# Loading the shared weight pieces of a recurrent memory transformer from a scratch with long rows

## The chip, the cores and the metric

The kernel runs on one core of one Trainium2 chip. The metric is the device time in microseconds of one execution; the median of three runs is given. Engines are named as in the profile: PE (TensorE, matmuls), PEld (its weight loads), DVE (VectorE), ACT (ScalarE), POOL (GpSimd), SP (SyncE, which here only issues transfers).

## The reference

Two branches are mixed by a gate. Branch A walks through the 2,048 tokens in 64 segments of 32; each segment attends to itself and to 8 memory rows, and the first 8 rows of its output are the next segment's memory, so that the segments form a chain. Branch B is a GEGLU layer.

```
g = sigmoid((x * gate_w).sum(-1))
for s in range(64):                       # branch A, Dm = 1024, 32 heads of 128
    h = concat([mem, x[32*s : 32*s+32]])  # 8 + 32 rows
    q, k, v = h @ Wq, h @ Wk, h @ Wv      # each 1024 x 4096
    p = softmax(mask(q k^T / sqrt(128)))
    o = (p v) @ Wo                        # 4096 x 1024
    mem, out_s = o[:8], o[8:]
b = (gelu(x @ w_gate) * (x @ w_up)) @ w_down
return g * a + (1 - g) * b
```

All tensors are in bfloat16. Wk, Wq, Wv and Wo hold 8 MB each, together 32 MB, which is more than the on-chip memory has: part of them has to be read again in every segment.

## The kernel before

**Steps and pieces.** A step is one segment. Each of the four weights is cut in 16 pieces of 512 KB, (m, u, i): m is the weight (k, q, v, o), u the half of the heads, i one of eight blocks (for k, q and v 128 rows of the contraction; for o a block of four heads and half of the columns). A piece fills one slot of 4,096 bytes in each of 128 partitions (`sl` for k, q, v, `wall` for o). A step does its projections in two rounds, r = 0 with half u = s % 2 and r = 1 with the other half; the next step starts with the half that this one ended with.

**Shared slots.** Most pieces have a slot of their own and are loaded once. Fourteen slots are shared by the two halves of a block (`PAIRS`, L313: k 0 and 1, q 0 and 1, v 0 to 4, o 0, 1, 4, 5, 6). A shared slot holds the half that r = 0 uses; when that use is over (`spent`, L440), the other half is loaded for r = 1 of the same step, and stays for r = 0 of the next. So each step loads 14 pieces, 7 MB.

**Loads in groups.** Where neighbouring slots come free together, one transfer loads them (`GROUPS`, L408: k 0-1, q 0-1, v 0-1, v 2-3, o 4-6); it goes out when the last of the group is spent (`load_group`, L420). Pieces of k, q and v come from the inputs, where a piece's row is 4,096 contiguous bytes of a row of 8,192. Pieces of Wo come from the input in rows of 1,024 bytes at first. In steps 1 to 10 `keep` (L383, called at L932) stores one shared piece of Wo in each step from its slot into a scratch in DRAM; from then on it is read from there, pieces 0 and 1 alone in rows of 4,096 bytes (`wo_scr`), pieces 4 to 6 as a group in rows of 12,288 (`wg_scr`).

**Order.** The order of the work is written out by hand. `walk` (L330) is the order of the projections: k0 (first half of its blocks), q0 (two), the second half of o1 of the step before, q0 (two), v0, k0, q0, v0, then k1, q1, o0, v1 and the first half of o1. `plan` (L899) hangs everything else on places of that list with `on(m, r, n, ...)`, which means: before block n of m in round r. At ("o", 1, 0) stand, among others, the attention of the second half, SP's load of qkr (rows of q and k of tokens that were projected ahead, L540) and SP's store of oRc (part of the attention's output, L985). All weights, hT (next inputs, L531), the stores of `keep` and these two go through SP's queue in program order, and an instruction of SP that waits holds those behind it. POOL issues smaller transfers on a queue of its own. Every instruction waits on semaphores that `_Prog` (L31) derives from which one writes and reads which bytes: a load into a slot waits for the last matmul that used it and for a store that reads it.

**Fills.** Rows that do not depend on the memory are projected ahead for four steps at a time (`fill`, L842, matmuls of L850): two such projections in each of two steps out of four, one in the two others, none in the last five. In steps with two, ACT copies the second result to a stage called 0S or 1S (L661), which lies on the same bytes as hT and oRc, so that this copy waits for the store of oRc to have landed.

**After step 63** the rest of Wo's products follow (L1027), and then branch B in four blocks of 512 tokens (L1068 on).

Of the kernel before, what the change touches and what calls it, by code (L numbers as in the profile page):

```python
# [5 lines left out]
BF16 = mybir.dt.bfloat16  # L6
# [24 lines left out]
class _Prog:  # L31
# [47 lines left out]
    def op(self, eng, fn, rd=(), wr=(), lane=None, after=()):  # L79
        o = _Op(eng, fn)  # L80
        if lane is not None:
            ln = self.lanes.get(lane)
            if ln is None:
                ln = self.lanes[lane] = [self.new_sem(f"{self.name}_{lane}"), 0, None]
            if ln[2] is not None:
                o.deps.append(ln[2])
            ln[1] += 16
            o.sem, o.val, o.inc, o.need = ln[0], ln[1], 16, True
            ln[2] = o
        for r in rd:  # L90
# [12 lines left out]
        return o  # L103
# [107 lines left out]
def bass_gated_mix__memory_aug_recurrent_mem_tr__geglu_ffn__prompt_kernel(  # L211
# [16 lines left out]
    S, D = xf.shape  # L228
# [17 lines left out]
    with ExitStack() as es:  # L246
# [14 lines left out]
        v_scr = nc.dram_tensor("v_scr", [NSEG, NB, 16, 2, 128], BF16)  # L261
        o_scr = nc.dram_tensor("o_scr", [NSEG, 128, 256], BF16)
        a_scr = nc.dram_tensor("a_scr", [NSEG, 4, SEG, 256], BF16)
        wo_scr = nc.dram_tensor("wo_scr", [16, 128, 2048], BF16)
        wg_scr = nc.dram_tensor("wg_scr", [2, 128, 3, 2048], BF16)

        PB = [es.enter_context(nc.psum_tensor(f"pb{i}", [128, 512], FP32)) for i in range(8)]
        PBV = [p[:, :].bitcast(BF16) for p in PB]
# [5 lines left out]
        def al(name, shape, dt=BF16, at=None):  # L274
            if at is None:
                cur[0] = (cur[0] + 63) // 64 * 64
                t = _T(nc, name, shape, dt, cur[0])
                cur[0] += t.nb
                return t
            return _T(nc, name, shape, dt, at)  # L280
# [32 lines left out]
        PAIRS = {"k": (0, 1), "q": (0, 1), "v": (0, 1, 2, 3, 4), "o": (0, 1, 4, 5, 6)}  # L313
# [33 lines left out]
        sl = al("sl", [128, nkqv, 2048])  # L347
# [11 lines left out]
        op = P.op  # L359
# [3 lines left out]
        def src(k):  # L363
            m, u, i = k
            if m == "o":
                h0 = 16 * u + 4 * (i % 4)
                return A_Wo[h0:h0 + 4, :, 512 * (i // 4):512 * (i // 4) + 512].rearrange("h p f -> p h f")
            W = {"q": A_Wq, "k": A_Wk, "v": A_Wv}[m]
            return W[i * 128:(i + 1) * 128, 16 * u:16 * u + 16, :].rearrange("d h e -> d (h e)")

        def dst(t, k):
            return t[:, :].rearrange("p (h f) -> p h f", h=4) if k[0] == "o" else t[:, :]

        kept = set()
        wo_at = lambda k: wg_scr[k[1], :, k[2] - 4, :] if 4 <= k[2] < 4 + 3 else wo_scr[8 * k[1] + k[2]]

        def load_piece(t, k, lane):
            if k in kept:
                op("sp", lambda e: e.dma_start(t[:, :], wo_at(k)), rd=[("D", "wo", k)], wr=[t.r()], lane=lane)
            else:  # L380
                op("sp", lambda e: e.dma_start(dst(t, k), src(k)), wr=[t.r()], lane=lane)

        def keep(k):  # L383
            t = slots[home[k]]
            op("sp", lambda e: e.dma_start(wo_at(k), t[:, :]), rd=[t.r()], wr=[("D", "wo", k)], lane="wo")
            kept.add(k)

        assert NSEG % 2 == 0
# [16 lines left out]
            if done[n] == 0 and uses[n][0] == k:  # L405
                fetch(n)

        GROUPS = {("k", 0): 2, ("q", 0): 2, ("v", 0): 2, ("v", 2): 2, ("o", 4): 3}  # L408
        lead = {(m, i + x): (m, i) for (m, i), n in GROUPS.items() for x in range(n)}
        for (m, i), n in GROUPS.items():  # L410
            assert all(home[m, 0, i + x] == home[m, 0, i] + x for x in range(n))
        held = {}

        def due(n):
# [5 lines left out]
        def load_group(k0, n):  # L420
            m, u, i = k0
            h = home[k0]
            t, x = (wall, h - nkqv) if m == "o" else (sl, h)
            reg = ("S", slots[h].off, slots[h].off + n * PIECE)
            if m == "o":
                op("sp", lambda e: e.dma_start(t[:, x:x + n, :], wg_scr[u]), rd=[("D", "wo", (m, u, i + y)) for y in range(n)],
                   wr=[reg], lane=f"sl{h}")
            else:
                W = {"q": A_Wq, "k": A_Wk, "v": A_Wv}[m]
                v = W[i * 128:(i + n) * 128, 16 * u:16 * u + 16, :].rearrange("(y p) h e -> p y (h e)", y=n)  # L430
                op("sp", lambda e: e.dma_start(t[:, x:x + n, :], v), wr=[reg], lane=f"sl{h}")
# [8 lines left out]
        def spent(k):  # L440
# [8 lines left out]
            q.append((n, *due(n)))  # L449
            if len(q) == GROUPS[g]:  # L450
                del held[g]
# [13 lines left out]
        for g in range(4):  # L465
            q = slice(32 * g, 32 * g + 32)
# [62 lines left out]
        def load_h(s, eng="sp"):  # L529
            t = hT[s % 2]  # L530
            op(eng, lambda e: e.dma_start(t[:, :, :].rearrange("p k c -> p (k c)"), xq_scr[s // 4, :, s % 4, :]),  # L531
               rd=[("D", "xq", s // 4)], wr=[t.r()], lane=f"h{eng}")
# [10 lines left out]
        def load_v(s, us=slice(0, 2), eng="pool"):  # L543
# [7 lines left out]
           wr=[gwb.r()], lane="gw")  # L551
# [3 lines left out]
        for n in range(8):  # L555
# [9 lines left out]
           rd=[memT.r()], wr=[hT0.r()])  # L565
# [328 lines left out]
        def fill0(m, r, b, st, G=0, h=hR):  # L894
            run(fill(m, r, b, h))
            fill_evac(m, r, G, b, st)
            fill_put(m, r, G, st)

        def plan(s):  # L899
            last = s == NSEG - 1  # L900
            ua, ub = s % 2, 1 - s % 2
# [6 lines left out]
            def on(m, r, n, *fs, s=s):  # L908
                at.setdefault((s, m, r, n), []).extend(fs)
# [18 lines left out]
                on("k", 0, 5, lambda: load_r(G))  # L928
            if not last and s == 0:
                on("k", 0, 4, lambda: load_h(s + 1))  # L930
            if 1 <= s <= 2 * len(PAIRS["o"]):
                on("k", 0, 4, lambda: keep(("o", s % 2, PAIRS["o"][(s - 1) // 2])))  # L932
            on("q", 0, 4, lambda: evac(bank_of["k", 0], stage["k"], "act"))
# [49 lines left out]
            if not last:  # L983
                on("o", 1, 0, lambda: load_qk(s + 1, 0, "sp"))
            on("o", 1, 0, lambda: op("sp", lambda e: e.dma_start(o_scr[s], oRc[:, :, :].rearrange("p c x -> p (c x)")),  # L985
                                     rd=[oRc.r()], wr=[("D", "o", s)], lane="sto"))
# [13 lines left out]
            if two:  # L1000
# [4 lines left out]
                                     wr=[("D", "a", s)], lane="st"), **nx)  # L1005

        for s in range(NSEG):
            plan(s)
        for _, e, m, r, n in walk:
# [6 lines left out]
           wr=[("D", "a", NSEG - 1)], lane="st")  # L1016

        load_oR(NBK - 1)
        for b in range(NBK):
            rb = rbs[b % 2]  # L1020
            for hf in range(2):
# [47 lines left out]
        for fb in range(NFB):  # L1069
            HB, DN = ((0, 1, 2, 3), (4, 5, 6, 7)) if fb % 2 == 0 else ((4, 5, 6, 7), (0, 1, 2, 3))  # L1070
            for j in range(NJ):
                c, cc = jch[j][0], jch[j][1] * 128
                bg, bu = HB[2 * (j % 2)], HB[2 * (j % 2) + 1]
                for bk, w in ((bg, wg[c]), (bu, wu[c])):
# [8 lines left out]
                t = tp[j % 2]  # L1083
# [4 lines left out]
                   rd=[BK(bg), s1.r()], wr=[t.r()])  # L1088
# [87 lines left out]
```

## Time and profile before

| | us |
|---|---|
| median of three runs | 2309.16 |
| lowest and highest | 2306.65, 2320.56 |
| the profiled execution, its own time | 2311.71 |
| its span, first to last instruction | 2309.9 |
| PE busy | 2069.2 |
| DVE busy | 1044.2 |
| ACT busy | 541.9 |
| POOL busy | 423.4 |
| first and last store of oRc (L985) | 124.1, 1657.8 |

The median of the runs is 0.1% below the profiled execution. A step is read from one store of oRc to the next. Median times from issue to landing: Wk's group 6.1 us, Wq's 9.0, Wv's 11.2, a single piece of Wo 6.2, Wo's group of three 9.5, the store of oRc 4.3. A transfer's time to landing holds its time in the queue; the time that it takes by itself is seen only where two land one behind the other. Besides the views that the prediction shows, the trace keeps a record of each packet that a DMA engine moved: queue, size and duration.

### The profile page before, as it was taken

What the parts mean: (1) busy time and instruction counts of PE and PEld (TensorE: products, weight loads), DVE (VectorE), ACT (ScalarE), POOL (GpSimd) and SP (SyncE); (2) the same over time, 40 slices, a digit from 0 to 9 for tenths busy, and PEclk for the clock granted to TensorE, in tenths of its full rate; (3) what the DMA queues carried; (4) which work ended last, traced back from release to release, by engine and by line L of the source; (5) the groups of instructions that cost most, each with busy time, mean ns of one, the idle gap of its engine ahead of it and who ended that gap; (6) DMA issues with size and microseconds to landing.
All of it is one profiled execution on the core that took longest, in us unless ns stands there. A gap on an engine that the chain in (4) does not pass through costs nothing.

```text
span 2309.9 us, 69920 instructions
## 1 busy us (share of the span) xinstructions
PE 2069.2 (90%) x31393; PEld 982.4 (43%) x31393; DVE 1044.2 (45%) x2697; ACT 541.9 (23%) x1111; POOL 423.4 (18%) x819
## 2 busy tenths in 40 slices
PE   4588888989999899898998989988799999999999
PEld 2243443444444444444444444443464444444444
DVE  3344444454444544445444444454315446163462
ACT  1122222222222222222222222221113123032130
POOL 4422212222222221222222222221100000000000
PEclk9699999999999999999999999998999999999999
DMA  9989999999999999999999989998964440803520
GB/s 370 358 299 336 327 337 347 324 341 334 330 346 328 347 322 327 344 318 352 322 340 339 331 313 328 324 344 313 331 214 139 153 148 10 291 19 128 167 88 19
DMA packets 237563, 638.04 MB, mean 276 GB/s; under 512 B 22441, under 2 KB 91305, under 8 KB 230481
## 3 DMA queue, kind: packets, MB, share of 16 engines
q1 hardware_dynamic: 213440, 596.58, 72.9%
q0 software_dynamic: 13888, 26.31, 3.5%
q10 hardware_dynamic: 9936, 10.69, 1.3%
q8 instruction: 247, 4.05, 0.7%
q14 instruction: 52, 0.42, 0.1%
HBM read 596.85 MB, written 36.63 MB: 274 GB/s over the span
## 4 chain that ended last, share of the span: by engine, by line
PE 56%; DMA 32%; DVE 5%; issue 3%; ACT 2%; POOL 1%; SPq 0%; ACTq 0%; POOLq 0%; DVEq 0%
PE pb L780 18%; PE pb L1077 15%; DMA sl<-in_A_Wv_dram 10%; DMA wall<-wg_scr 7%; PE pb L1131 5%; DMA qkr<-qk_scr 3%; PE pb L813 3%; DMA o_scr<-oRc 3%; PE pb L796 3%; PE pb L678 3%; PE pb L850 3%; PE pb L1027 2%; PE pb L1112 2%; DMA sl<-in_A_Wq_dram 1%; DMA xr_scr<-xr 1%
## 5 line engine op out<-in xcount | busy, mean ns | idle before, releaser
L780 PE MATMUL pb<-sl,hT 128*32 128x512 bf16 x12288 | 776.1, 385 | 36.6 <-DMA sl<-in_A_Wv_dram 17.3
L780 PEld LDWEIGHTS pb<-sl,hT 128*32 128x32 bf16 x12288 | 312.5, 97 | 361.4 <-DMA sl<-in_A_Wv_dram 39.8
L850 PE MATMUL pb<-sl,hR 128*32 128x512 bf16 x3072 | 220.7, 392 | 3.5 <-issue 2.9
L1077 PE MATMUL pb<-xT,wg 128*128 128x512 bf16 x896 | 211.7, 379 | 0.8
L1077 PE MATMUL pb<-xT,wu 128*128 128x512 bf16 x896 | 211.7, 379 | 0.0
L813 PE MATMUL pb<-wall,oT 128*32 128x256 bf16 x4056 | 154.1, 278 | 33.7 <-DMA wall<-wg_scr 10.5
L824 DVE COPY part<-pb 64x256 f32<-64x256 f32 x128 | 54.0, 422 | 256.8 <-PE pb L813 256.0
L661 ACT ACTIVATE kS<-pb 128x512 bf16<-128x512 f32 x127 | 75.8, 597 | 385.1 <-PE pb L780 363.7
L796 PE MATMUL pb<-wall,oT 128*32 128x512 bf16 x2048 | 150.4, 389 | 9.8 <-issue 2.9
L763 POOL COPY oRc<-oT 128x128 bf16<-128x128 bf16 x128 | 96.3, 752 | 339.9 <-DVE oT L664 336.8
L1131 PE MATMUL pb<-wd,GT 128*128 128x512 bf16 x672 | 146.6, 379 | 2.7 <-DMA wd<-in_B_w_down_dram 2.6
L1085 ACT ACTIVATE s<-pb 128x512 f32<-128x512 f32 x112 | 66.8, 596 | 313.4 <-PE pb L1077 313.4
L813 PEld LDWEIGHTS pb<-wall,oT 128*32 128x32 bf16 x4056 | 96.9, 97 | 95.8 <-ACT oT L661 25.8
L714 ACT ACTIVATE E<-pb 128x320 bf16<-128x320 f32 x128 | 56.0, 437 | 333.8 <-DVE pb L713 333.8
L1086 DVE SCALAR_TENSOR_TENSOR tp<-s,pb 128x512 f32<-128x512 f32 x112 | 76.9, 687 | 125.9 <-ACT s L1085 125.7
L1077 PEld LDWEIGHTS pb<-xT,wg 128*128 128x128 bf16 x896 | 87.2, 98 | 107.9 <-DVE GT L1093 3.7
L1077 PEld LDWEIGHTS pb<-xT,wu 128*128 128x128 bf16 x896 | 87.7, 98 | 105.7
L879 POOL COPY kT<-qkr 128x128 bf16<-128x128 bf16 x128 | 37.3, 291 | 491.0 <-DVE kT L664 229.4
L664 DVE COPY kT<-pb 128x512 bf16<-128x512 bf16 x128 | 54.4, 425 | 160.9 <-PE pb L678 160.9
L664 DVE CAST oT<-pb 128x160 bf16<-128x160 f32 x256 | 76.5, 320 | 104.4 <-PE pb L746 104.4
L726 DVE STREAM_TRANSPOSE tAB<-pAB 128x128 bf16<-128x128 bf16 x512 | 114.0, 280 | 4.4
L1090 DVE SCALAR_TENSOR_TENSOR tp<-tp,pb 128x512 f32<-128x512 f32 x112 | 77.0, 687 | 78.5 <-ACT tp L1089 78.5
(103 smaller groups left out, 2158.6 us busy)
## 6 DMA issues: line engine op xcount, KB each, us to landing
sl<-in_A_Wv_dram SPq DMA_DIRECT2D x128, 1024.0 KB, 11.2
wall<-wg_scr SPq DMA_DIRECT2D x53, 1536.0 KB, 9.5
sl<-in_A_Wk_dram SPq DMA_DIRECT2D x64, 1024.0 KB, 6.1
sl<-in_A_Wq_dram SPq DMA_DIRECT2D x64, 1024.0 KB, 9.0
wall<-wo_scr SPq DMA_DIRECT2D x120, 512.0 KB, 6.2
wd<-in_B_w_down_dram SPq DMA_DIRECT2D x42, 1024.0 KB, 5.5
sl<-in_A_Wv_dram SPq DMA_DIRECT2D x75, 512.0 KB, 11.4
wall<-in_A_Wo_dram SPq DMA_DIRECT2D x41, 512.0 KB, 7.9
```

The source lines that it names most:

```text
L661: op("act", lambda e: e.activation(o, i, ACTF.Copy), rd=rd, wr=wr)
L664: op("dve", lambda e: e.tensor_copy(o, i), rd=rd, wr=wr, after=after)
L726: return [op("dve", lambda e, c=c: e.transpose(tAB[:, c + 32 * k:c + 32 * k + 4 * w].rearrange("p (j x) -> p j x", j=4)[:, :, 0:32], pAB[: ...
L763: op("pool", lambda e: e.tensor_copy(oRc[:, :, 16 * u:16 * u + 16].rearrange("p c x -> p x c"), oT[:, :, :, 32:40].rearrange("p g j c -> p ...
L780: ins = e.matmul(PB[bk][32 * g:32 * g + 32, :], lhsT=h[:, i, :], rhs=w[:, g * 512:(g + 1) * 512], start=(n == 0), stop=(n == 7))
L796: ins = e.matmul(PB[XO][32 * g:32 * g + 32, :], lhsT=oT[:, j, x, 0:32], rhs=wall[:, na:nb + 1:nb - na, c:c + 256], start=(n == 0 and hp == 0),
L813: ins = e.matmul(PB[XO][32 * g:32 * g + 32, 256 * b:256 * b + 256], lhsT=oT[:, j, x, 0:32], rhs=w[:, c:c + 256], start=False, stop=(n % 4 ...
L850: ins = e.matmul(PB[b][32 * g:32 * g + 32, :], lhsT=h[:, k[2], :], rhs=w[:, g * 512:(g + 1) * 512], start=(n == 0), stop=(n == 7))
L1077: ins = e.matmul(PB[bk][:, 0:FB], lhsT=w[:, kc, cc:cc + 128], rhs=xT[:, :, :, kc, :].rearrange("p t i c -> p (t i) c"), start=(kc == 0), s ...
L1086: op("dve", lambda e, hg=hg, t=t: e.scalar_tensor_tensor(out=t[:, :], in0=s1[:, :], scalar=1.0, in1=hg, op0=ALU.add, op1=ALU.mult), rd=[BK ...
L1090: op("dve", lambda e, hu=hu, t=t: e.scalar_tensor_tensor(out=t[:, :], in0=t[:, :], scalar=1.0, in1=hu, op0=ALU.add, op1=ALU.mult), rd=[BK( ...
L1131: ins = e.matmul(PB[bank[2 * k + hf]][:, :], lhsT=GT[:, j, tb * 128:(tb + 1) * 128], rhs=w[:, jj, hf * 512:(hf + 1) * 512], start=(j == 0) ...
```

## The change

The two scratches of Wo give way to one scratch for each group of shared pieces, laid out so that a group's row is contiguous: 8,192 bytes for groups of two (k 0-1, q 0-1, v 3-4, o 0-1), 12,288 for groups of three (v 0-2, o 4-6). All 14 shared slots are now in a group. Besides the 10 stores of Wo, which stay where they are, a shared piece of k, q or v is stored in each of the steps 3 to 20, as the first thing at ("o", 1, 0): v in steps 3 to 12, k in 13 to 16, q in 17 to 20, each piece's two halves in two successive steps. A group is loaded from its scratch once all its pieces of that half are there, and from the input before. The v groups are cut otherwise: 0 to 2 and 3 to 4 in place of 0-1, 2-3 and 4 alone; o 0 and 1 are loaded together.

```diff
-        wo_scr = nc.dram_tensor("wo_scr", [16, 128, 2048], BF16)
-        wg_scr = nc.dram_tensor("wg_scr", [2, 128, 3, 2048], BF16)
...
+        GROUPS = {("k", 0): 2, ("q", 0): 2, ("v", 0): 3, ("v", 3): 2, ("o", 0): 2, ("o", 4): 3}
+        lead = {(m, i + x): (m, i) for (m, i), n in GROUPS.items() for x in range(n)}
...
+        run_scr = {g: nc.dram_tensor(f"{g[0]}{g[1]}_scr", [2, 128, n, 2048], BF16) for g, n in GROUPS.items()}
         kept = set()
-        wo_at = lambda k: wg_scr[k[1], :, k[2] - 4, :] if 4 <= k[2] < 4 + 3 else wo_scr[8 * k[1] + k[2]]
+
+        def at_scr(k):
+            g = lead[k[0], k[2]]
+            return run_scr[g][k[1], :, k[2] - g[1], :]
 
         def load_piece(t, k, lane):
             if k in kept:
-                op("sp", lambda e: e.dma_start(t[:, :], wo_at(k)), rd=[("D", "wo", k)], wr=[t.r()], lane=lane)
+                op("sp", lambda e: e.dma_start(t[:, :], at_scr(k)), rd=[("D", "w", k)], wr=[t.r()], lane=lane)
...
         def keep(k):
             t = slots[home[k]]
-            op("sp", lambda e: e.dma_start(wo_at(k), t[:, :]), rd=[t.r()], wr=[("D", "wo", k)], lane="wo")
+            op("sp", lambda e: e.dma_start(at_scr(k), t[:, :]), rd=[t.r()], wr=[("D", "w", k)], lane="wo")
             kept.add(k)
...
-        GROUPS = {("k", 0): 2, ("q", 0): 2, ("v", 0): 2, ("v", 2): 2, ("o", 4): 3}
...
-            if m == "o":
-                op("sp", lambda e: e.dma_start(t[:, x:x + n, :], wg_scr[u]), rd=[("D", "wo", (m, u, i + y)) for y in range(n)],
-                   wr=[reg], lane=f"sl{h}")
+            ks = [(m, u, i + y) for y in range(n)]
+            if all(k in kept for k in ks):
+                op("sp", lambda e: e.dma_start(t[:, x:x + n, :], run_scr[m, i][u]), rd=[("D", "w", k) for k in ks], wr=[reg], lane=f"sl{h}")
...
+        STORE = [(m, i) for m in "vkq" for i in PAIRS[m]]
...
+            if 3 <= s < 3 + 2 * len(STORE):
+                on("o", 1, 0, lambda: keep((STORE[(s - 3) // 2][0], ub, STORE[(s - 3) // 2][1])))
             if 1 <= s <= 2 * len(PAIRS["o"]):
                 on("k", 0, 4, lambda: keep(("o", s % 2, PAIRS["o"][(s - 1) // 2])))
```

More of the change, by code (lines that the diff above doesn't have):

```diff
@@ L372, in dst @@
             return t[:, :].rearrange("p (h f) -> p h f", h=4) if k[0] == "o" else t[:, :]
+        GROUPS = {("k", 0): 2, ("q", 0): 2, ("v", 0): 3, ("v", 3): 2, ("o", 0): 2, ("o", 4): 3}
+        lead = {(m, i + x): (m, i) for (m, i), n in GROUPS.items() for x in range(n)}
+        for (m, i), n in GROUPS.items():
+            assert all(home[m, 0, i + x] == home[m, 0, i] + x for x in range(n))
+        run_scr = {g: nc.dram_tensor(f"{g[0]}{g[1]}_scr", [2, 128, n, 2048], BF16) for g, n in GROUPS.items()}
         kept = set()
-        wo_at = lambda k: wg_scr[k[1], :, k[2] - 4, :] if 4 <= k[2] < 4 + 3 else wo_scr[8 * k[1] + k[2]]
+        def at_scr(k):
+            g = lead[k[0], k[2]]
+            return run_scr[g][k[1], :, k[2] - g[1], :]
         def load_piece(t, k, lane):
             if k in kept:
-                op("sp", lambda e: e.dma_start(t[:, :], wo_at(k)), rd=[("D", "wo", k)], wr=[t.r()], lane=lane)
+                op("sp", lambda e: e.dma_start(t[:, :], at_scr(k)), rd=[("D", "w", k)], wr=[t.r()], lane=lane)
             else:
@@ L406, in first @@
                 fetch(n)
-        GROUPS = {("k", 0): 2, ("q", 0): 2, ("v", 0): 2, ("v", 2): 2, ("o", 4): 3}
-        lead = {(m, i + x): (m, i) for (m, i), n in GROUPS.items() for x in range(n)}
-        for (m, i), n in GROUPS.items():
-            assert all(home[m, 0, i + x] == home[m, 0, i] + x for x in range(n))
         held = {}
```

## The prediction

> **What bounds the kernel now.** I read the page first: busy shares, slices, DMA queues and the chain that ended last.
>
> ```profile
> PE 2069.2 (90%) x31393; PEld 982.4 (43%) x31393; DVE 1044.2 (45%) x2697; ACT 541.9 (23%) x1111; POOL 423.4 (18%) x819
> ...
> DMA  9989999999999999999999989998964440803520
> ...
> q1 hardware_dynamic: 213440, 596.58, 72.9%
> ...
> PE 56%; DMA 32%; DVE 5%; issue 3%; ACT 2%; POOL 1%; SPq 0%; ACTq 0%; POOLq 0%; DVEq 0%
> ```
>
> TensorE and the DMA engines are both about full until 1,660 us, where the 64 recurrent steps end. A step runs here from one store of oRc (L985) to the next. Busy time by stretches comes next (columns: stretch, length, PE, PEld, DVE, ACT, POOL, clock, DMA share, GB/s): steps 1 to 9, 10 to 57, and the five that have no fills.
>
> ```profile
> 148.90:382.10 233.20, 200.33 (x4002) 94.20 (x4002) 103.83 (x315) 55.12 (x122) 55.09 (x113) 0.98 0.96 335
> 382.10:1536.80 1154.70, 1046.39 (x21224) 498.61 (x21216) 553.48 (x1680) 293.06 (x648) 289.20 (x589) 0.99 0.93 332
> 1536.80:1657.80 121.00, 98.52 (x1966) 47.89 (x1958) 55.55 (x170) 25.98 (x60) 21.71 (x49) 0.94 0.92 329
> ```
>
> Per step that is 25.9, 24.1 and 24.2 us, with DMA busy for 24.9, 22.4 and 22.3 us and PE for 22.3, 21.8 and 19.7 us. The last five have 2 us less PE work and are no shorter: a step follows its transfers. The first nine load Wo in 1,024-byte rows and store a piece each: 2.5 us more DMA, 1.8 us more step. So 1 us of DMA is worth about 0.75 us. How much faster transfers can give at most, the waits of PE from 400 to 1560 us (48 steps) tell:
>
> ```profile
> PE pb L703 <- POOL kT L879: 12.0, 13, 3.2
> PE pb L813 <- DMA wall<-wg_scr: 10.0, 15, 1.4
> PE pb L780 <- DMA sl<-in_A_Wv_dram: 7.3, 16, 0.7
> PE pb L813 <- DMA wall<-wo_scr: 6.5, 11, 1.2
> ...
> PE pb L780 <- DMA sl<-in_A_Wq_dram: 5.0, 5, 1.7
> ...
> PE pb L678 <- ACT 1S L661: 4.0, 10, 1.0
> ```
>
> Weights: 28.8 us. The first row waits for qkr, a transfer too; ACT's copies 1S and 0S (1.0 us) wait for the store of oRc. In all 46 us, or 0.95 us a step: beyond that PE is the bound. Last, SyncE's issues around one seam of two steps:
>
> ```profile
> 1142.10 0.32 SPq L426 DMA_DIRECT2D wall<-wg_scr  x1
> 1142.46 0.43 SPq L540 DMA_DIRECT2D qkr<-qk_scr  x1
> 1147.37 0.32 SPq L985 DMA_DIRECT2D o_scr<-oRc  x1
> 1151.14 0.38 SPq L431 DMA_DIRECT2D sl<-in_A_Wk_dram  x1
> 1152.00 0.38 SPq L431 DMA_DIRECT2D sl<-in_A_Wq_dram  x1
> ```
>
> The Wk load goes out 9.0 us after the grouped Wo load, when the queue is nearly drained. At this seam the DMA share dips, by 1.3 us a step on average.
>
> **The rows.** A full step loads 14 pieces of 128 rows. Before, 11 are in rows of 4,096 bytes and three in rows of 12,288: 1,408 + 128 = 1,536 packets. After, four groups of two and two of three: 768 packets. The trace's packet records (main queue, 400 to 1650 us) give 4,096 bytes at 159 ns median and 185.5 mean, 12,288 at 460 and 485.6; 512 at 27, and 1,024 in the first steps at 46. The medians lie on one line, 8.4 ns a packet plus 0.0368 ns a byte, so 8,192 bytes would take 310 ns, a size no record shows. Fixed part saved: 768 x 8.4 ns / 16 engines = 0.40 us a step. If the stalls above the median (26 ns in both sizes) also go by packets, 8,192 bytes take 335.5 ns, and the saving is 128 x (3 x 185.5 - 485.6) / 16 = 0.57 us for the three Wv pieces plus 4 x 128 x (371 - 335.5) / 16 = 1.14 us, together 1.70. For stalls that go by bytes speak rows of one phase of the step: 3.5 ns above the median for 1,024 bytes, 12 for 4,096, 9 to 22 for 12,288. Transfers that land one behind another agree: 2.81 us per MiB of Wv, 4.13 us for 1.5 MiB of wg_scr, 2% apart. I take 0.6 us, near the lower end; ends 0 (rows of 8,192 bytes at a power-of-two pitch gain nothing) and 1.70. At 0.75 that is 0.45 us of step, under the cap of 0.95. In shares of the saving: steps 5 to 8 have one sixth (the Wo pair), 9 to 12 a half, 13 to 16 two thirds, 17 to 20 five sixths: 8.7 steps' worth; with 42 full steps, 50.7 x 0.45 = **-22.8 us**.
>
> The Trainium skill ("DMA: Bandwidth & Descriptors", Why small descriptors are slow) speaks against this gain: about three cycles of overhead a packet, at the page's 850 MHz 3.5 ns. By that estimate 768 packets are worth 0.17 us, the term is -6 us and the sum about 2329 us. The 8.4 ns of the records disagree, so the row decides.
>
> **The stores.** One 512 KB store in each of steps 3 to 20: 128 packets of 4,096 bytes, which took 163 ns in the stores of Wo: 1.3 us of DMA. In steps 3 to 10 a Wo store runs too and the queue is full: 8 x 1.3 x 0.75 = **+7.8**. In steps 11 to 20 the store stands right behind the grouped Wo load, where the queue dips anyway by 1.3 us; I take 0.5 each, between 0 and 1.3: **+5**. A Wv store waits on SyncE for the piece to land, up to 2 us behind the Wo group (Wv lands at 1144.2); behind it wait qkr and the store of oRc, which SyncE anyhow issues 5 us later. On the queue both lie behind the 1.3 us, and ACT's copy 1S or 0S, which waits for that store, is late in the nine steps of the stretch that have two fills. Half of 9 x 0.8: **+3.5**, ends 0 and 12.
>
> **The wait for a store's landing.** A stored piece is overwritten by the next step's load. For Wk (steps 13 to 16) the store ends at best 0.4 us of issue, 9.5 us of wg_scr, 1.3 us and its receipt after 1142.1, about 1153.4; the load had gone at 1151.14. SyncE is held over 2 us, with Wq and Wv queued behind, and the queue is empty. 4 x 1.5 beyond the 0.5 above: **+6**, ends 0 and 12. For Wq and Wv, loads of 3 us and more are queued in front: nothing.
>
> **Coarser groups.** Wv piece 3 now waits for piece 4 (3.2 us later), Wo piece 0 for piece 1 (1.0 to 1.5 us later). Both hide behind the queue: 3.5 MiB lie ahead of the first, and Wv, which lands 20 us after the store of oRc, ahead of the second, whose issue 17.5 us after it needs 1.07 us to its first packet. 0.05 us in 60 steps: **+3**, ends 0 and 18. Issues saved on SyncE (two a step, 0.34 us each) are worth nothing, as it waits most of the time. The 630 us of the other stage are untouched.
>
> Sum: 7.8 + 5 + 3.5 + 6 + 3 - 22.8 = +2.5 us on the profiled execution's 2311.7 (span 2309.9) gives 2314.2; the median of the runs is 2.5 lower than that execution, so **2312 us**: no change. A measurement can tell about 1%, 23 us.
>
> **Rivals.** (1) Stalls go with packets: 1.70 us of DMA, of which PE can use some 0.85: -43 us, and stores that sink into the dip at 18: 2309 - 43 + 18 = 2284. For it: equal stalls in both sizes over the whole stage. Against: the landings. (2) Slower: the stores are not covered. The place is the seam: each of the 18 holds the main queue 1.3 us and ACT's copies or the next loads 1.0 more, 41 us, and Wk waits 3 us four times, 12. With 3 for groups and -22.8: 2309 + 33 = 2342. It decides once a store step costs 2.5 us more than now. For it: a queue at 0.96 in steps 3 to 10; against: the dip. (3) Longer packets hold the engines: the POOL queue's qkr, 16 packets on 16 engines, each waits 460 instead of 159 ns for its turn. 0.3 x 43 steps on top: 2326. PE's 12.0 us behind kT speaks for it, but they were 13 times in 48 steps, and that queue's 4,096-byte packets took 189 ns mean against 159 median: waiting is there, but short. [...] (4) Rows are split into 4,096 again and nothing is gained: 2335; the 12,288-byte packets speak against it.
>
> **Numbers.** Forecast 0.57, (1) 0.18, (2) 0.17, (3) 0.05, (4) 0.03. Faster by over 1% (under 2286): 0.16, most of (1). Slower by over 1% (over 2332): 0.20, (2) and (4). Within: 0.64. The range 2286 to 2338 leaves out about half of (1) and of (2).
>
> **What would show it.** Main-queue packets fall by about 37,000 (50.7 x 768, less 18 x 128 stored). 8,192-byte records near 310 to 335 ns; steps 21 to 57 at 23.6 us; steps 3 to 10 at 26.4 instead of 25.4, 13 to 16 over 25, with SyncE at the Wk load waiting for a k store. PE's waits for weights fall from 28.8 us towards 10. Wrong if steps from 21 on stay at 24.1 (rows give nothing) or fall under 23.2 (stalls go with packets), or if the store steps add over 40 us.

## The result and the profile after

| | before | after |
|---|---|---|
| median of 20 runs each, us | 2308.76 | 2322.81 |
| lowest and highest | 2300.22, 2320.56 | 2309.04, 2332.30 |
| the profiled execution (span) | 2311.71 (2309.9) | 2315.04 (2313.2) |

The ratio is 1.0062 (95%: 1.0048 to 1.0077). The change costs 14 us: within the 1% that was called "no change", but with 20 runs it is seen. The profiled execution of after lies 7.8 us under its median, so its trace shows only part of the loss.

The page of after, with the lines that answer to those shown of before:

```profile
PE 2066.6 (89%) x31368; PEld 988.2 (43%) x31393; DVE 1044.6 (45%) x2697; ACT 541.8 (23%) x1111; POOL 425.0 (18%) x819
...
DMA  9999999988998988899898999898964440803520
...
q1 hardware_dynamic: 174384, 606.02, 71.8%
...
PE 59%; DMA 29%; DVE 5%; issue 2%; ACT 2%; POOL 1%; SPq 0%; ACTq 0%; POOLq 0%
```

The main queue moves 9.4 MB more (the 18 stores) in 39,056 packets fewer, and takes a smaller share of the span. The DMA row has ten eights in its first 28 slices, where before had three: the engines are less full and the kernel is no faster. Where the time is shows by stretches (columns as in the prediction): steps 3 to 10, 11 and 12, 13 to 20, which hold the stores, then 21 to 57 and the last five.

```profile
202.30:413.40 211.10, 179.30 (x3538) 83.42 (x3535) 92.24 (x280) 48.75 (x108) 48.47 (x100) 0.97 0.97 342
413.40:463.20 49.80, 43.35 (x880) 20.38 (x880) 23.51 (x71) 12.18 (x27) 9.98 (x21) 1.00 0.95 338
463.20:674.20 211.00, 180.40 (x3557) 84.91 (x3560) 92.30 (x280) 48.77 (x108) 48.48 (x100) 0.96 0.89 324
674.20:1545.60 871.40, 800.15 (x16354) 389.89 (x16346) 426.97 (x1295) 226.10 (x500) 224.85 (x456) 0.99 0.90 340
1545.60:1662.20 116.60, 97.39 (x1958) 46.88 (x1962) 55.57 (x170) 25.98 (x60) 21.45 (x49) 0.94 0.90 343
```

Divided by the number of steps (from one store of oRc to the next; steps 13 to 20 split by the trace), with the same for before and for the experiments, one execution each:

| us a step | 3-10 | 11-12 | 13-16 | 17-20 | 21-57 | 58-62 |
|---|---|---|---|---|---|---|
| before | 25.40 | 23.60 | 24.07 | 23.93 | 24.12 | 24.21 |
| after | 26.38 | 24.94 | 27.05 | 25.69 | 23.55 | 23.40 |
| e1, no stores of k, q, v | 25.52 | 23.99 | 23.77 | 24.17 | 24.50 | 23.78 |
| e2, store moved | 25.51 | 24.61 | 27.06 | 24.62 | 23.87 | 23.31 |
| e3, long rows from the inputs | 24.44 | 23.58 | 23.34 | 24.06 | 23.99 | 23.47 |
| e8, scratch rows of 4,096 | 26.73 | 25.93 | 26.72 | 25.88 | 23.76 | 23.48 |
| f1, only the Wv groups | 25.10 | 23.33 | 24.46 | 23.91 | 23.63 | 23.56 |
| f2, only the Wo pair | 25.68 | 24.25 | 24.24 | 24.84 | 25.01 | 24.66 |
| f3, scratch with old groups | 26.30 | 23.70 | 26.42 | 24.92 | 23.04 | 22.64 |
| f5, stores alone | 26.92 | 25.00 | 26.18 | 24.83 | 23.86 | 23.92 |
| m1, change less the Wo pair | 25.87 | 23.85 | 26.21 | 25.46 | 23.37 | 23.06 |
| g1, m1 with stores moved | 25.64 | 23.48 | 24.63 | 24.45 | 23.28 | 23.62 |
| h1, f1 with k and q singly | 24.60 | 23.46 | 23.33 | 24.19 | 23.56 | 23.19 |
| h4, Wo together but single | 25.25 | 25.69 | 25.36 | 24.17 | 24.52 | 24.83 |

From step 21 on e2 does the same work as after, and the two differ by 0.3 us there: one profiled execution tells no more than that. Differences of a few tenths are judged by the timed ratios only.

Steps 3 to 20 became 29.4 us longer, steps 21 to 57 20.9 us and 58 to 62 4.1 us shorter. The waits of PE in the store steps, before (199 to 644.5 us) and after (202 to 674 us); columns: us in total, times, longest:

```profile
PE pb L780 <- DMA sl<-in_A_Wv_dram: 10.2, 9, 2.0
...
PE pb L678 <- ACT 1S L661: 1.7, 5, 0.7
PE pb L678 <- ACT 0S L661: 1.5, 3, 0.8
```

```profile
PE pb L815 <- DMA wall<-o_scr: 11.4, 14, 1.7
...
PE pb L680 <- ACT 1S L663: 9.6, 4, 3.3
...
PE pb L680 <- ACT 0S L663: 7.3, 5, 1.9
```

ACT's copies held PE 3.2 us before and 16.9 us after. They wait for the store of oRc to land, and that is late. The line of that store in the store steps (before 199 to 644 us, after 202 to 674 us) (issue to landing in us, smallest, median, largest):

```profile
DMA to landing us min/median/max: 3.6/4.3/7.6
```

```profile
DMA to landing us min/median/max: 4.4/7.0/8.3
```

From step 21 on the median in after is 4.5 again. The second thing in these steps is SyncE, here after's issues around a seam of step 13, where a piece of Wk is stored:

```profile
457.96 0.32 SPq L429 DMA_DIRECT2D wall<-o_scr  x1
458.32 0.43 SPq L391 DMA_DIRECT2D k_scr<-sl  x1
458.80 0.64 SPq L542 DMA_DIRECT2D qkr<-qk_scr  x1
463.23 0.32 SPq L991 DMA_DIRECT2D o_scr<-oRc  x1
470.16 0.38 SPq L433 DMA_DIRECT2D sl<-in_A_Wk_dram  x1
```

The Wk load goes out 6.9 us after the store of oRc (3.8 us at the seam of before that the prediction shows). It overwrites the piece that is being stored, and waits; Wq and Wv queue behind it. SyncE's waits in after name all three:

```profile
SPq L143 <- DMA k_scr<-sl: 23.8, 4, 6.5
...
SPq L143 <- DMA q_scr<-sl: 13.2, 4, 4.4
...
SPq L143 <- DMA v_scr<-sl: 10.5, 5, 3.2
```

(Steps 13 to 16, with the k stores, are 3.0 us a step longer than before; steps 17 to 20, with the q stores, 1.8.)

In steps 21 to 57 the waits of PE for weights went from 23.5 us, before:

```profile
PE pb L813 <- DMA wall<-wg_scr: 8.0, 12, 1.4
PE pb L703 <- POOL kT L879: 7.6, 9, 3.2
PE pb L780 <- DMA sl<-in_A_Wv_dram: 6.0, 13, 0.7
PE pb L813 <- DMA wall<-wo_scr: 5.5, 10, 1.2
...
PE pb L780 <- DMA sl<-in_A_Wq_dram: 4.0, 4, 1.7
```

to 13.2 us, all of it now at Wo, after:

```profile
PE pb L815 <- DMA wall<-o_scr: 13.2, 18, 1.9
PE pb L705 <- POOL kT L881: 11.4, 17, 1.2
```

So the loads of k, q and v stopped being late, as they were meant to, and Wo did not. By the order in which SyncE issued what PE waits for, the 13.2 us are 5.7 for the pair and 7.5 for the group of three; before, 5.5 were for the second single piece, none for the first, and 8.0 for the group. A seam of after shows when the pair goes out, by stretches of 1 us and by SyncE's issues (store of oRc at 1146.78):

```profile
1162.78:1163.78 1.00, 0.94 (x13) 0.26 (x11) 0.66 (x2) 0.00 (x0) 0.00 (x0) 1.00 0.77 303
1163.78:1164.78 1.00, 0.00 (x0) 0.00 (x0) 0.00 (x0) 0.00 (x0) 0.29 (x1) 1.00 0.52 123
1164.78:1165.78 1.00, 0.95 (x36) 0.67 (x40) 0.52 (x2) 0.00 (x0) 0.82 (x2) 1.00 0.48 164
```

```profile
1162.03 0.32 SPq L533 DMA_DIRECT2D hT<-xq_scr  x1
1163.76 2.21 SPq L429 DMA_DIRECT2D wall<-o_scr  x2
```

and a seam of before (store of oRc at 1147.37):

```profile
1163.37:1164.37 1.00, 0.99 (x13) 0.40 (x13) 0.38 (x2) 0.62 (x3) 0.00 (x0) 1.00 0.98 393
1164.37:1165.37 1.00, 0.64 (x9) 0.12 (x8) 0.65 (x2) 0.00 (x0) 0.00 (x0) 1.00 1.05 389
1165.37:1166.37 1.00, 0.48 (x24) 0.40 (x28) 0.00 (x0) 0.00 (x0) 0.76 (x2) 1.00 1.11 326
```

In before the engines stay full through this stretch (0.98 to 1.11). In after they are half empty (0.52, 0.48) for two microseconds, until the pair that is issued at 1163.76 starts to move. PE's idle microsecond there isn't the pair's: it ends with kT, which waits for qkr (1.1 us; 0.9 us at this place of before), and no wait for Wo follows at this seam. In the mean over steps 21 to 57, counted from the store of oRc, before issues the first single Wo load at 16.35 us, when the last of Wv has yet to land at 20.8; after issues the pair, which waits for the second piece to be used, at 17.2, and Wv lands at 19.1. Nine tenths of the packets of that last Wv load have ended 2 us before it lands, and the engines run short from 17 us on. The DMA share 16 to 20 us behind the store is 0.70 to 0.76 after, and 0.97 to 1.00 before.

### The profile page after: what moved, and what is told of

Same layout as the page of the kernel before. It is cut to its first block, busy times and chain, and to the rows that moved or that the text cites. A ratio compares the mean times of both kernels' runs of the same rounds, so it can differ in the third digit from the quotient of the medians.

```text
span 2313.2 us, 69748 instructions
## 1 busy us (share of the span) xinstructions
PE 2066.6 (89%) x31368; PEld 988.2 (43%) x31393; DVE 1044.6 (45%) x2697; ACT 541.8 (23%) x1111; POOL 425.0 (18%) x819
## 4 chain that ended last, share of the span: by engine, by line
PE 59%; DMA 29%; DVE 5%; issue 2%; ACT 2%; POOL 1%; SPq 0%; ACTq 0%; POOLq 0%
PE pb L782 20%; PE pb L1083 15%; DMA wall<-o_scr 10%; PE pb L1137 5%; DMA o_scr<-oRc 4%; DMA qkr<-qk_scr 4%; PE pb L798 3%; PE pb L680 3%; DMA sl<-in_A_Wv_dram 3%; PE pb L815 3%; PE pb L1033 2%; PE pb L1118 2%; PE pb L852 2%; DMA xr_scr<-xr 1%; DMA wall<-in_A_Wo_dram 1%
```

## The experiments

Each ratio is to the kernel before on the same chip, with its 95% interval; 1% is 23 us. Diffs are against the changed kernel; "no stores" means the line of e1.

**e1: the change without its 18 stores.** Groups of k, q and v stay on the inputs; Wo's pair and group stay on the scratch.

```diff
-        STORE = [(m, i) for m in "vkq" for i in PAIRS[m]]
+        STORE = []
```

> The changed kernel without its 18 stores of Wk, Wq and Wv: these groups stay on the inputs in rows of 4,096 bytes, cut 0-2 and 3-4 for Wv, and only the pair of Wo gets rows of 8,192. My theory (the 18 store steps cost some 29 us, long rows give some 25 back, coarser groups next to nothing): the store cost is gone and so is most of the gain, about 0.1 us a step is left from the Wo pair, ratio to before 0.998 (0.995 to 1.001), steps 21 to 57 at 24.0 us. Rival, the coarser groups hold loads back: ratio over 1.004, steps of 24.4 us and more in all stretches.

Measured: 1.0110 (1.0083 to 1.0136). That is past the rival's mark of 1.004. What is left when the stores and the long rows of k, q and v are gone is 25 us slower than before: the regrouping, which the prediction had at +3. Its waits from 670 to 1545 us are at Wo:

```profile
PE pb L815 <- DMA wall<-o_scr: 26.7, 26, 2.4
```

against 13.5 us for Wo before (8.0 and 5.5 above).

**e2: the store behind the store of oRc.** The call of `keep` for k, q and v moves from the head of ("o", 1, 0) to behind L985.

```diff
-            if 3 <= s < 3 + 2 * len(STORE):
-                on("o", 1, 0, lambda: keep((STORE[(s - 3) // 2][0], ub, STORE[(s - 3) // 2][1])))
...
                                     rd=[oRc.r()], wr=[("D", "o", s)], lane="sto"))
+            if 3 <= s < 3 + 2 * len(STORE):
+                on("o", 1, 0, lambda: keep((STORE[(s - 3) // 2][0], ub, STORE[(s - 3) // 2][1])))
```

> The changed kernel with the stores of Wk, Wq and Wv issued just behind the store of oRc and not ahead of it. My theory (a good part of the cost is that oRc's store lands 2.5 us later behind the 512 KB, and ACT's copies 0S and 1S wait for it in the steps with two fills): those nine steps get shorter by 1.5 to 2 us, ratio to before 0.999 (0.996 to 1.002). Rival, the cost is the stores' own DMA time and the wait of the Wk load: no change from the changed kernel, 1.006.

Measured: 1.0026 (1.0010 to 1.0041), half way between the two. PE's waits for ACT's copies in the store steps fall to 6.1 us (2.8 and 3.3), steps 3 to 10 to 25.51 us; steps 13 to 16 stay at 27.06, as the Wk load waits as before (22.3 us on SyncE). So the place of the store is worth 0.36% or 8 us (1.0062 less 1.0026), ACT's part; the wait of Wk is a second one.

**e3: long rows without a store.** The groups of k, q and v read contiguous stretches of the inputs, 8 or 12 KB a partition, that are not their blocks (the same stretch in every step).

```diff
-                v = W[i * 128:(i + n) * 128, 16 * u:16 * u + 16, :].rearrange("(y p) h e -> p y (h e)", y=n)
-                op("sp", lambda e: e.dma_start(t[:, x:x + n, :], v), wr=[reg], lane=f"sl{h}")
+                v = W[64 * i:64 * i + 64 * n, :, :].rearrange("d h e -> (d h e)").rearrange("(p f) -> p f", p=128)
+                op("sp", lambda e: e.dma_start(t[:, x:x + n, :].rearrange("p y f -> p (y f)"), v), wr=[reg], lane=f"sl{h}")
...
-        STORE = [(m, i) for m in "vkq" for i in PAIRS[m]]
+        STORE = []
```

> Long rows with no stores of Wk, Wq and Wv: their groups are read from contiguous stretches of the inputs in rows of 8,192 and 12,288 bytes, which are not the rows that the step needs, so what is computed from them is left wrong; bytes, groups and issues are those of the changed kernel. My theory (rows are worth 0.57 us a step, and nothing else of the change matters once the stores are gone): 60 steps, -33 us, ratio 0.986 (0.982 to 0.990). Rival, the gain seen after step 20 comes from the scratch's place or from the stretch itself: ratio 0.995 or more.

Measured: 0.9909 (0.9880 to 0.9938), a little short of the expected range. Against e1, which has the same regrouping, that is 0.0201, 46 us, for all k, q and v groups: about twice the 22.8 us forecast (they also act in steps 1 to 20, without stores). The rows are longer here and lie contiguous too; e8 takes the two apart.

**e8: the same scratch with rows of 4,096 bytes.** A piece lies contiguous in the scratch, and a group of n reads n rows of 4,096 per partition.

```diff
-        run_scr = {g: nc.dram_tensor(f"{g[0]}{g[1]}_scr", [2, 128, n, 2048], BF16) for g, n in GROUPS.items()}
+        run_scr = {g: nc.dram_tensor(f"{g[0]}{g[1]}_scr", [2, n, 128, 2048], BF16) for g, n in GROUPS.items()}
...
-            return run_scr[g][k[1], :, k[2] - g[1], :]
+            return run_scr[g][k[1], k[2] - g[1]]
...
-                op("sp", lambda e: e.dma_start(t[:, x:x + n, :], run_scr[m, i][u]), rd=[("D", "w", k) for k in ks], wr=[reg], lane=f"sl{h}")
+                op("sp", lambda e: e.dma_start(t[:, x:x + n, :], run_scr[m, i][u].rearrange("y p f -> p y f")), rd=[("D", "w", k) for k in ks], wr=[reg], lane=f"sl{h}")
```

> The changed kernel with its scratches laid out piece by piece, so that every row is 4,096 bytes, Wo's group of three too; stores, groups, issues and order are the same. My theory (the gain from step 21 on is the length of the rows): steps 21 to 57 at 24.1 to 24.3 us instead of 23.55, ratio to before 1.017 (1.013 to 1.021). Rival, the gain comes from reading a contiguous scratch or from fewer transfers: 1.006, steps at 23.6 us.

Measured: 1.0098 (1.0077 to 1.0120), between the expected 1.017 and the rival's 1.006. Against the change that is 0.36%, 8 us (2 to 14), for the length of the rows alone, those of Wo's group of three included. The larger part of what the scratch brings stays with rows of 4,096 bytes. The loads show it too: KB each and median time from issue to landing over the whole run, before, e8 and after.

```profile
sl<-in_A_Wk_dram SPq DMA_DIRECT2D x64, 1024.0 KB, 6.1
sl<-in_A_Wq_dram SPq DMA_DIRECT2D x64, 1024.0 KB, 9.0
```

```profile
sl<-k_scr SPq DMA_DIRECT2D x47, 1024.0 KB, 5.3
sl<-q_scr SPq DMA_DIRECT2D x43, 1024.0 KB, 7.9
```

```profile
sl<-k_scr SPq DMA_DIRECT2D x47, 1024.0 KB, 5.5
sl<-q_scr SPq DMA_DIRECT2D x43, 1024.0 KB, 7.7
```

**f1: before, with only the Wv groups changed** (0 to 2 and 3 to 4, read from the input; no stores, Wo singly).

```diff
-        GROUPS = {("k", 0): 2, ("q", 0): 2, ("v", 0): 3, ("v", 3): 2, ("o", 0): 2, ("o", 4): 3}
+        GROUPS = {("k", 0): 2, ("q", 0): 2, ("v", 0): 3, ("v", 3): 2, ("o", 0): 1, ("o", 1): 1, ("o", 4): 3}
...
-        STORE = [(m, i) for m in "vkq" for i in PAIRS[m]]
+        STORE = []
```

> The kernel before with only Wv's groups cut as in the change (0-2 and 3-4), in rows of 4,096 bytes from the input; Wo's pieces 0 and 1 alone as before, no stores of Wk, Wq and Wv. My revised theory (the groups cost 1.1% in the run without stores, and it is the pair of Wo: PE's wait for it went from 5.5 to 21.6 us in steps 21 to 57): ratio 1.000 (0.997 to 1.004). Rival, Wv's groups cost it: 1.008 or more.

Measured: 0.9889 (0.9866 to 0.9911). Theory and rival both missed: the coarser Wv groups gain 26 us by themselves.

**f2: before, with only the Wo pair** (no stores, Wv groups as before; the pair has rows of 8,192 bytes).

```diff
-        GROUPS = {("k", 0): 2, ("q", 0): 2, ("v", 0): 3, ("v", 3): 2, ("o", 0): 2, ("o", 4): 3}
+        GROUPS = {("k", 0): 2, ("q", 0): 2, ("v", 0): 2, ("v", 2): 2, ("v", 4): 1, ("o", 0): 2, ("o", 4): 3}
...
-        STORE = [(m, i) for m in "vkq" for i in PAIRS[m]]
+        STORE = []
```

> The kernel before with only Wo's pieces 0 and 1 made a group with rows of 8,192 bytes; Wv's groups as before, no stores of Wk, Wq and Wv. Revised theory: the first of the two pieces is asked for 1 to 1.5 us later and both land together, PE waits for the pair some 15 us more in steps 21 to 57, ratio 1.009 (1.005 to 1.013). Rival, Wv's groups: 1.000.

Measured: 1.0216 (1.0186 to 1.0245), 50 us lost, more than twice what was expected. f1 and f2 add up to e1: -1.11 + 2.16 = 1.05% against 1.10%. Waits of PE in f2 (670 to 1545 us) and in f1:

```profile
PE pb L815 <- DMA wall<-o_scr: 30.7, 24, 2.6
...
PE pb L705 <- POOL kT L881: 13.6, 15, 2.0
```

```profile
PE pb L815 <- DMA wall<-o_scr: 3.1, 6, 1.3
```

In f2 the pair is issued 18.1 us after the store of oRc and lands at 25.1, in the mean; before, the singles landed at 22.35 and 23.80. PE needs the first piece first, and gets it 2.8 us later. Its waits for the pair are 29.7 us in steps 21 to 57, by SyncE's order of issue. The queue isn't dry here: the DMA share 16 to 20 us behind the store of oRc is 0.97, and 0.98 before.

**f3: the change with the groups of before** (all 18 stores; rows of 8 KB for k, q and two pairs of v).

```diff
-        GROUPS = {("k", 0): 2, ("q", 0): 2, ("v", 0): 3, ("v", 3): 2, ("o", 0): 2, ("o", 4): 3}
+        GROUPS = {("k", 0): 2, ("q", 0): 2, ("v", 0): 2, ("v", 2): 2, ("v", 4): 1, ("o", 0): 1, ("o", 1): 1, ("o", 4): 3}
```

> The change with the groups of before: scratches for k 0-1, q 0-1, v 0-1, v 2-3 (rows of 8,192 bytes), v 4, o 0 and o 1 alone (4,096) and o 4-6 (12,288); all 18 stores as in the change. Revised theory (coarser groups cost little where rows are fast, since the Wo pair then lands in time, 5.7 us of waits): steady steps of 23.6 us, ratio to before 1.003 (0.999 to 1.007). Rival, the groups cost the change over 20 us as they do without stores: 0.996 or less.

Measured: 0.9943 (0.9924 to 0.9962): the rival's mark. The revised theory failed: in the change the regrouping costs 1.19% (1.0062 less 0.9943), 27 us.

**f5: the stores alone.** As f3, but what is stored of k, q and v is never read.

```diff
-            kept.add(k)
+            if k[0] == "o":
+                kept.add(k)
```

> The kernel before with its groups, plus the 18 stores of Wk, Wq and Wv to scratches that are never read: the price of the stores by itself. Theory: steps 3 to 20 some 30 us longer, of them two-fill steps most, steps from 21 on at 24.1 as before; ratio 1.014 (1.010 to 1.018). My forecast priced them at 22 us, 1.010; rival, stores that hide in the dip of the queue: 1.005.

Measured: 1.0083 (1.0055 to 1.0112), less than the theory and near the forecast: the stores cost 19 us (13 to 26). f3 less f5 is what reading from the scratch brings with the groups of before: -1.40%, 32 us.

**m1: the change with Wo 0 and 1 loaded singly.**

```diff
-        GROUPS = {("k", 0): 2, ("q", 0): 2, ("v", 0): 3, ("v", 3): 2, ("o", 0): 2, ("o", 4): 3}
+        GROUPS = {("k", 0): 2, ("q", 0): 2, ("v", 0): 3, ("v", 3): 2, ("o", 0): 1, ("o", 1): 1, ("o", 4): 3}
```

> The change with one part undone: Wo's pieces 0 and 1 are loaded alone, as soon as each is spent, in rows of 4,096 bytes; all else, the 18 stores among it, is as changed. If the terms add up (the pair alone cost 2.2%, the change gave 1.0062): ratio 0.985 (0.981 to 0.990), the dry stretch of the queue 16 to 20 us after oRc's store is filled, steps 21 to 57 at 22.9 us. Rival, long rows ahead make the pair land in time, so that it costs the change little: 0.998 or more.

Measured: 0.9937 (0.9915 to 0.9958), 0.9% short of the expected 0.985. Without the Wo pair the change is faster than before; the pair costs 1.25% or 29 us in it. But m1 equals f3: the Wv groups, which gain 1.1% on the input, gain nothing on the scratch. The profiles of m1 and after have nearly the same total of waits for Wo in steps 21 to 57 (12.4 and 13.2 us), so the pair's price inside the change rests on the timed ratios, not on that row. The DMA share 16 to 20 us behind the store of oRc is 0.85 in m1 and 0.73 after: the dry stretch is filled in part.

**g1: m1 with the stores moved.** The store of v goes behind the store of oRc, that of k in front of block 0 of Wk in r = 1, that of q in front of block 0 of Wq in r = 1.

```diff
-            if 3 <= s < 3 + 2 * len(STORE):
-                on("o", 1, 0, lambda: keep((STORE[(s - 3) // 2][0], ub, STORE[(s - 3) // 2][1])))
+            if 13 <= s < 3 + 2 * len(STORE):
+                on("k" if s < 17 else "q", 1, 0, lambda: keep((STORE[(s - 3) // 2][0], ub, STORE[(s - 3) // 2][1])))
...
+            if 3 <= s < 13:
+                on("o", 1, 0, lambda: keep((STORE[(s - 3) // 2][0], ub, STORE[(s - 3) // 2][1])))
```

> The former with the stores at other places: Wv's behind the store of oRc, Wk's at the start of k1 and Wq's at the start of q1 of the same step, where the pieces have just landed and the load that overwrites them is a step away. My theory (the cost of the stores is the two waits, of ACT for oRc's store and of the Wk load, more than their DMA time): steps 13 to 20 near 24 us, steps 3 to 12 some 0.6 us shorter than in the former, 0.5 to 0.8% less than the former, 0.979 (0.975 to 0.984). Rival, a store costs its 1.3 us of DMA wherever it stands: within 0.2% of the former.

Measured: 0.9898 (0.9877 to 0.9919). Less than expected, but the store steps 13 to 16 fall from 26.21 to 24.63 us. SyncE's only wait for a store of these weights that is left is

```profile
SPq L143 <- DMA v_scr<-sl: 9.1, 5, 2.5
```

and PE waits for ACT's copies 5.0 us from 200 to 670 us, where m1 had 17.5. The place of the stores is worth 0.39%, 9 us; the two intervals together leave 0.1 to 0.7%, so the rival's 0.2% isn't ruled out by the times alone.

**h1: f1 with Wk and Wq as single pieces.** The question was whether a pair of the input is slow because its two blocks lie 1 MiB apart.

```diff
-        GROUPS = {("k", 0): 2, ("q", 0): 2, ("v", 0): 3, ("v", 3): 2, ("o", 0): 2, ("o", 4): 3}
+        GROUPS = {("k", 0): 1, ("k", 1): 1, ("q", 0): 1, ("q", 1): 1, ("v", 0): 3, ("v", 3): 2, ("o", 0): 1, ("o", 1): 1, ("o", 4): 3}
...
-        STORE = [(m, i) for m in "vkq" for i in PAIRS[m]]
+        STORE = []
```

> The kernel before with Wv's groups of the change (which gave 0.989) and Wk's and Wq's pairs cut into single pieces of 128 rows of 4,096 bytes from the input; no stores of Wk, Wq and Wv. It tells where the slow reads of Wk and Wq come from (340 GB/s with all engines busy, 5 to 11 us after oRc's store, against 390 from a scratch). If it is the pair, whose two rows a partition lie 1 MB apart in the input: 390 GB/s there, packets of 4,096 bytes near 165 ns, ratio 0.982. If it is the place (the half rows of the input, or the time behind the dry seam): 340 GB/s again, 0.988 to 0.992.

Measured: 0.9885 (0.9858 to 0.9912), the same as f1. 8 to 10 us after the store of oRc the engines move 343 GB/s (f1 338): single pieces are read no faster, so the pair's pattern isn't it.

**h4: Wo 0 and 1 as two transfers, both issued at the time of the pair.** Groups of before otherwise, no stores.

```diff
-        GROUPS = {("k", 0): 2, ("q", 0): 2, ("v", 0): 3, ("v", 3): 2, ("o", 0): 2, ("o", 4): 3}
+        GROUPS = {("k", 0): 2, ("q", 0): 2, ("v", 0): 2, ("v", 2): 2, ("v", 4): 1, ("o", 0): 2, ("o", 4): 3}
...
+            if g == ("o", 0):
+                return run_scr[g][k[1]].rearrange("p n f -> (p n f)").rearrange("(n p f) -> n p f", n=2, p=128)[k[2]]
...
-            if all(k in kept for k in ks):
+            if (m, i) == ("o", 0):
+                for k in ks:
+                    op("sp", lambda e, k=k: e.dma_start(slots[home[k]][:, :], at_scr(k)), rd=[("D", "w", k)], wr=[slots[home[k]].r()],
+                       lane=f"sl{home[k]}", after=[next(o for o in reversed(P.ops) if o.eng == "pe")])
+            elif all(k in kept for k in ks):
...
-        STORE = [(m, i) for m in "vkq" for i in PAIRS[m]]
+        STORE = []
```

> The kernel before with Wo's pieces 0 and 1 as two transfers in rows of 4,096 bytes, each landing by itself, but both issued when the second is spent. It tells apart what costs in the pair. If it is the late issue (the queue runs dry and the first piece lands late): ratio 1.015 to 1.022 like the pair. If it is that two pieces land as one: 1.005 or less.

Measured: 1.0127 (1.0108 to 1.0146), between the two marks. The late issue alone costs 1.27 of the pair's 2.16%. The pieces land at 23.3 and 24.7 us behind the store of oRc, 0.9 us later than before each, and PE's waits for Wo in steps 21 to 57 double from 13.5 to 27.5 us: 2.7 for the first piece, 12.0 for the second, 12.8 for the group of three behind them. The rest of the 2.16% goes with the two pieces being one transfer, whose first half can't be used before its second has landed; that part was not tried by itself.

## Why the prediction was right in the time, and where it was wrong

Three kernels in a row split the 14 us (they add up by construction): stores +19 (f5), reading from the scratch -32 (f3 less f5), regrouping +27 (the change less f3). The prediction had +22.3, -22.8 and +3. The time came out near because the second error (-9) and the third (+24) have opposite signs; that part was luck.

- **The rows: right in sign, too small, and in the main for another reason.** The median of 8,192-byte packets is 309 ns, as the line said (310), and 12,288 bytes stay at 460. But the length of the rows brings only 8 us (e8, with the new groups) where the scratch brings 32 (with the old ones). The rest is that packets stall less from the scratch: means over 680 to 1540 us are 185.3 ns for 4,096 bytes before and 174.7 in e8 from the scratch; after, 8,192 bytes take 349.2, just twice 174.7. So stalls went neither by packets nor by bytes, the two cases that were weighed: they went with where and how the data lie, and with the time in the step too, for Wo's single pieces, read from a scratch in 4,096-byte rows, had a mean of 198.7 ns in m1. 1,408 packets x 10.6 ns / 16 engines are 0.93 us of DMA a step, more than the 0.6 taken for the whole term. With the groups of before, counts times means give 20.1 us a step for f5 and 19.3 for f3: 0.8 us, which at 0.75 and in 50.7 steps is 30 us, near the 32 timed. So the DMA time saved was mis-sized, and the factor 0.75 held.
- **The stores: right in sum.** +19 (13 to 26) against 22.3. Steps 3 to 10 came at 26.38 us (forecast 26.4), steps 13 to 16 at 27.05 ("over 25"), with SyncE at the Wk load behind the k store. Inside the term ACT was mis-sized: 3.5 us forecast, 13.7 us more of PE's waits measured; "ends 0 and 12" was just too low. "Nothing" for Wq was too low as well: with its store moved, steps 17 to 20 fall from 25.46 (m1) to 24.45 us (g1).
- **The coarser groups: the step that failed.** "Both hide behind the queue" gave +3, ends 0 and 18. The Wo pair costs 50 us alone and 29 in the change. The cover was Wv, "which lands 20 us after the store of oRc". Three things were wrong with it. The landing was taken for the end of the packets, most of which are through about 2 us earlier (seen in after), so that even at the old pace the cover was just used up (20.8 - 2 = 18.8 us against an issue at 17.5 and 1.07 us to the first packet). It was read from a kernel whose loads were slow: from the scratch Wv lands at 19.1, the engines run short from 17 us, and the change has removed its own cover. And a full queue was no cover to begin with: in f2, at a share of 0.97, the first piece lands with the second, 2.8 us later, and PE waits 29.7 us for the pair; the forecast priced the later issue alone. h4 shows the issue to be the larger half. In the profile of after PE waits only 5.7 us for the pair in steps 21 to 57, so by what path it costs 29 us there is shown in part at most: some 12 us go with a lower clock (last section).
- **The Wv groups** were costed at nothing and gain 26 us on the input, nothing on the scratch. The rates below show a part of it; why is open.
- **The rivals.** (1) Stalls by packets: refuted, for from the scratch packets of 4,096 bytes stand 16 ns above their median (e8) and those of 8,192 bytes 40 ns (after). (2) Stores not covered, from 2.5 us a store step: the store steps cost 29.4 us over 18, 1.6 each, regrouping included. (3) Longer packets against qkr: PE behind kT went from 7.6 to 11.4 us in steps 21 to 57, but was 4.3 in f3 and 8.9 in g1, which have long packets too; a few us at most, not 0.3 x 43 = 13. (4) Rows split: refuted by 39,056 packets fewer (forecast 37,000).
- **What would show it.** Steps 21 to 57 at 23.55 (forecast 23.6) looked like a full hit, and is the sum of two errors: 23.04 without the regrouping (f3).

A better version follows: g1 (0.9898) keeps the scratch without the Wo pair and with stores where nothing waits for them. It beats both kernels by 1.0 and 1.6%, but f1 (0.9889), which adds no scratch of k, q or v at all and only cuts Wv's groups otherwise, is as fast.

What stays open: by what path the pair costs the rest of its 29 us in the change, why half-rows of the inputs are read more slowly 6 to 12 us behind the store of oRc, and why groups of three blocks of Wv are read faster from them than pairs.

## What to carry to other kernels

Before you join two loads that fall due 1 us apart, ask when the first piece lands with and without the join, and take the cover from the kernel as it will be, not as it is: a change that speeds the queue empties it. Price each regrouping by a run of its own. Before you credit a gain to row length, run the same new layout with short rows; and put a large store behind the small store that others wait for.

## What the runs showed of the hardware

**Where a read comes from mattered more than its row length.** With the engines' share at 0.99 to 1.01, the mean rate in steps 21 to 57, 6 to 8, 8 to 10 and 10 to 12 us after the store of oRc, was 332, 341 and 360 GB/s before (half-rows of the inputs), 382, 382 and 379 in e8 (scratch, rows of 4,096 bytes) and 388, 395 and 392 after (rows of 8 and 12 KB). Contiguous stretches of the inputs themselves (e3) gave 362, 371 and 385 at shares of 0.93 to 1.00: it is no property of the scratch. 12 to 14 us after it, where Wv is read, a group of three blocks on the input ran at 406 (f1), 405 (h1) and 393 (e1), a pair at 357 (before) and 352 (f2); on the scratch, 421 (after) and 419 (f3), groups or pairs. The Trainium skill ("DMA: Bandwidth & Descriptors", Latency and other measured facts) lists lower rates for tiles whose rows lie 512 KiB or more apart, and advises contiguous tiles. The rows here lie 8 KB apart and the blocks of a pair 1 MiB; contiguous layouts were faster here too, but h1's single pieces, which have no second block, were not, so no run here shows that this is the cause.

**A bigger transfer was the dearer one.** The Trainium skill (same page, Measured, under Bandwidth) asks for 1 MiB or more in a transfer, measured there on transfers issued from GpSimd; these go out from SyncE. Joining two 512 KB loads into 1 MiB cost 2.16% in f2: in a queue that is filled anyway, the earlier issue and landing were worth more.

**After waits of PE its clock was halved for 3.4 or 6.8 us.** Steps 21 to 57 of f3, before and f2 (columns as in the prediction), with the same matmuls but for a few records:

```profile
666.02:1518.61 852.59, 794.60 (x16371) 388.11 (x16362) 426.55 (x1295) 226.34 (x500) 224.46 (x456) 1.00 0.93 348
```

```profile
644.46:1536.76 892.30, 808.95 (x16378) 386.15 (x16378) 426.66 (x1295) 226.23 (x500) 224.02 (x456) 0.99 0.93 332
```

```profile
655.15:1580.57 925.42, 819.07 (x16370) 393.01 (x16370) 426.52 (x1295) 226.09 (x500) 224.23 (x456) 0.98 0.90 320
```

Of the 72.8 us between the first and the last, 48.3 are idle time of PE and 24.5 its busy time: a sum over waits, as the prediction makes it, misses a third. The trace's records of the granted clock show where. In these steps it stands at 0.5 in nine stretches of f2, together 44.4 us, in three of before (13.7 us) and in none of f3. At half the clock 44.4 us do the work of 22, which is most of the 24.5; for before against f3 it is 7 of 14. In the 4 us ahead of each of f2's nine stretches PE had idled 1.6 to 3.4 us. One of them follows a wait for the pair:

```profile
1079.64 0.89 PE L815 MATMUL pb<-wall,oT 128*32 128x256 bf16 x16 [2.04 <-DMA wall<-o_scr]
...
1084.60 1.92 PE L815 MATMUL pb<-wall,oT 128*32 128x256 bf16 x32
```

```profile
1079.86:1086.69 6.83, 5.59 (x78) 2.67 (x73) 1.13 (x4) 0.00 (x0) 0.89 (x2) 0.50 0.69 226
```

The 32 matmuls take 1.92 us here, and 1.06 us at the full clock (after, at 1169.89 us). So a late load can cost more than the wait that it causes. The mean granted clock of all timed runs bears it out: 0.970 in f2 and 0.979 in before on that chip, 0.976 in after and 0.980 in m1. One less the clock, times the run's time, bounds what this can take; it grows by 24 of f2's 50 us, and by 12 of the 29 us between m1 and after. No run changed the clock by itself, and how much idle time it takes was not measured.
